# Attention features and an ELU block on one core: unread products at the start, one-bank tiles for h, and two token groups that take the weight pairs in turns

## The chip, the cores and the metric

The kernel runs on one core of one Trainium2 chip. The metric is the device time of one execution in microseconds (us). A core has five engines that run their own instruction streams: TensorE (PE in the rows; its weight loads are PEld), VectorE (DVE), ScalarE (ACT), GpSimd (POOL) and SyncE (SP, which here only issues transfers). Each works in the order in which its instructions stand, and waits on semaphores for the others.

## What is computed

The reference, cut to what matters (float64 weights `moe_w_in`, `moe_w_out`, `S1`, `S2`; q, k, v in float32):

```python
# batch, heads, seq, head_dim = 4, 4, 1088, 32;  r = 8;  d_model = 128, d_ff = 2048
def phi(x):
    a = einsum('rd,bhsd->bhsr', S1, x); b = einsum('rd,bhsd->bhsr', S2, x)
    return einsum('bhsi,bhsj->bhsij', a, b).reshape(..., r * r)
q_p, k_p = phi(q), phi(k)
kv  = einsum('bhsf,bhsd->bhfd', k_p, v);   z = sum(k_p, axis=s)
num = einsum('bhsf,bhfd->bhsd', q_p, kv);  den = einsum('bhsf,bhf->bhs', q_p, z) + 1e-06
x = (num / den) as (4352 tokens, 128)
h = x @ w_in
out = where(h > 0, h, exp(min(h, 0)) - 1) @ w_out
```

## The kernel before, in words

The 4352 tokens are 68 half tiles of 64; eight half tiles are a group of 512 tokens, so there are nine groups (0 to 8), the last with 256 tokens. Groups 0 and 1 belong to batch 0. `NP = 8` weight pairs (`cp`) hold 256 columns of `w_in` and the 256 rows of `w_out` that belong to them.

**The head** (code ahead of the list `steps`) loads k, q and v of batch 0, makes the features of k (`KF`, `KO`), sums k features times v into the PSUM tile `kv` (`KA`), makes the features of group 0 (`q1_first`, `q2_first`, `q4_first`) and the normalised x of group 0 (`q5_first`, tile `xg`). `q5_first` copies `kv` with its sum column into `kvz` (ScalarE), runs 16 products of 64 rows, one per head (`x0ps`), then DVE divides by the denominator (`dn`, `xn`), TensorE transposes (`x0tp`), and ScalarE and DVE copy one half of `xg` each. `keep_warm` issues a 128x128 product of the identity with itself into the tile `idle`, which nothing reads; six of them stand in `q5_first`.

**The weights** are float64 in DRAM. They land as pairs of 32-bit words in `raw` and are rounded to float32 by `round_a` (DVE), `round_b` (ScalarE) and `round_c` (four DVE instructions, or two DVE and two GpSimd with `pool=True`). `RA`, `RB`, `RC` do that for entry i of the list `order`: an entry is (pair, w_in?, w_out?). Before, the first four pairs are rounded in halves of 256 columns.

**The steps.** `seg` lists which group takes which pairs one after the other: before, group 0 takes pairs 0 to 3, group 1 pairs 0 to 3, group 0 pairs 4 to 7, group 1 pairs 4 to 7, and then each later group takes all eight. Step n is one (group, pair): `mm1` (two products of 512 tokens into the PSUM tile `h`, two banks, two buffers), `elu` (ScalarE: relu of -h, then exp, tile `e`; DVE: max(h, e - 1), tile `gg`), and two steps later `mm2` (two products accumulated in the PSUM tile `o`). When a stretch of pairs of a group ends, `fin1` copies `o` to `oT` or adds it there (DVE); after the last pair `fin2` transposes and stores. `at(n, ...)` puts other work after `mm1` of step n, `late(n, ...)` after `elu` of step n: rounding of the next weights, and for group g the steps `q1` (features and denominators, one PSUM tile), `q2` (DVE), `q4` (transposes, copied by ScalarE to `qpT`) and `q5` (products with `kvS`, copied to `xg`), and for each batch the k work. `KZ1` and `KZ2` fold a batch's sum of k features into the weights `SW` that `q1` of this batch needs; `KS` copies `kv` to `kvS`.

Each engine's program order is the order of this code. Transfers are issued by SP in the code's order, two of them and v of batch 0 by ScalarE.

Of the kernel before, what the change touches and what calls it, by code (L numbers as in the profile page):

```python
# [27 lines left out]
def kernel(  # L28
# [56 lines left out]

    ebias = const.tile([P, 1], F32, name="ebias")
# [18 lines left out]
    def round_c(raw, dst, pool=False):  # L105
        lo, hi = raw[:, :, 0], raw[:, :, 1]
# [3 lines left out]
        mant = lo.bitcast(F32)  # L110
        nc.vector.scalar_tensor_tensor(mant, lo, 2.0 ** -32, hi, op0=MUL, op1=ADD)  # L111
# [23 lines left out]
    load_v(nc.scalar, 0)  # L135
# [18 lines left out]
    order = [(0, 1, 0), (1, 1, 0), (2, 1, 0), (0, 0, 1), (3, 1, 0), (1, 0, 1), (2, 0, 1), (3, 0, 1)]  # L154
    order += [(cp, 1, 1) for cp in range(NP // 2, NP)]
# [25 lines left out]
    for b in range(1, B):  # L181
# [44 lines left out]
    kvz = const.tile([P, 2, D + 1], F32, name="kvz")  # L226
# [50 lines left out]
    def KZ1(b):  # L277
# [74 lines left out]

    WARM = 4, 2
    idle = psum.tile([P, 512], F32, name="idle", tag="o", bufs=1)

    def keep_warm():
        nc.tensor.matmul(idle[:, :P], ident[:], ident[:], skip_group_check=True)
# [28 lines left out]
    def q5_first():  # L386
        nc.scalar.copy(kvz[:], kv_ps[0][:, :, :D + 1])
# [8 lines left out]
        for i in range(WARM[0]):  # L396
            keep_warm()
# [17 lines left out]
        for i in range(WARM[1]):  # L415
            keep_warm()
# [231 lines left out]
```

## Time and profile before

| | |
|---|---|
| three runs | 320.78, 322.21, 322.82 us; median 322.21 |
| the profiled execution | 321.12 us, of which the profile's span is 318.6 us |
| TensorE busy | 296.2 us (93% of the span) |
| DVE, ScalarE, GpSimd busy | 160.4, 177.1, 22.5 us |
| mean granted TensorE clock | 0.989 of full speed |

Times in the rows are us from the span's start. A row of the timeline is: start, how long, engine, line, operation, out<-in tiles, shape, count of merged instructions, and in brackets how long the engine was idle before it and what released it. One float32 product is two TensorE rows, so "x4" of h or o is two products; a transpose is one row. The end of a TensorE row is modelled and lies beyond the start of the next one.

### The profile page before, as it was taken

How to read it: one execution, taken by the hardware profiler on the slowest of the kernel's cores; microseconds unless marked ns; L12 is line 12 of the kernel's file. 1: busy time of each engine (PE TensorE's matmuls, PEld its weight loads, DVE VectorE, ACT ScalarE, POOL GpSimd, SP SyncE). 2: the span in 40 equal slices, each digit the busy share in tenths (PEclk: the TensorE clock that was granted, in tenths of full speed). 3: DMA queues.
4: the chain of work that ended last, by engine and by line, in shares of the span. 5: the costliest groups of instructions: out<-in, count | busy, mean ns of one | idle time of the engine just before them, and what ended most of it. 6: DMA issues, size and time to landing. Idle time of an engine off the chain costs nothing. (4 is left out here: it accounts for less than half of the span.)

```text
span 318.6 us, 3773 instructions
## 1 busy us (share of the span) xinstructions
PE 296.2 (93%) x1498; PEld 151.3 (47%) x1498; DVE 160.4 (50%) x236; ACT 177.1 (56%) x237; POOL 22.5 (7%) x36
## 2 busy tenths in 40 slices
PE   2997769997999999999999999999999999999993
PEld 2863223543454444544554455444544444444682
DVE  5846865994533365446233645626333624443431
ACT  2326665554566565466655663566565565566561
POOL 2000014647000000000000000000000000000000
PEclk9997999997999999999999999999999999999999
DMA  6921189502001010000100010001000100010010
GB/s 187 337 83 30 39 228 255 146 0 70 0 2 33 0 33 2 0 2 0 34 2 0 0 33 2 0 2 34 0 2 0 33 0 0 2 33 0 0 35 16
DMA packets 9184, 13.34 MB, mean 42 GB/s; under 512 B 912, under 2 KB 6544, under 8 KB 9168
## 3 DMA queue, kind: packets, MB, share of 16 engines
q1 hardware_dynamic: 8336, 12.29, 14.0%
q10 hardware_dynamic: 832, 0.82, 0.9%
q8 instruction: 12, 0.20, 0.3%
q14 instruction: 4, 0.03, 0.0%
HBM read 10.88 MB, written 2.23 MB: 41 GB/s over the span
## 5 line engine op out<-in xcount | busy, mean ns | idle before, releaser
L473 DVE SCALAR_TENSOR_TENSOR gg<-e,h 128x1024 f32<-128x1024 f32 (+1 forms) x74 | 83.8, 1133 | 128.2 <-ACT e L472 123.6
L482 PE MATMUL o<-gg,W 128*128 128x512 f32 (+1 forms) x288 | 133.1, 585 | 4.0 <-POOL W L114 2.7
L460 PE MATMUL h<-xg,W 128*128 128x512 f32 (+1 forms) x288 | 130.4, 576 | 2.9 <-DVE gg L473 2.2
L471 ACT ACTIVATE e<-h 128x1024 f32<-128x1024 f32 (+1 forms) x74 | 70.9, 958 | 52.1 <-PE h L460 45.4
L460 PEld LDWEIGHTS h<-xg,W 128*128 128x128 f32 x288 | 54.3, 192 | 63.1 <-issue 61.7
L482 PEld LDWEIGHTS o<-gg,W 128*128 128x128 f32 x288 | 52.5, 192 | 57.5 <-issue 46.4
L472 ACT ACTIVATE e<-e 128x1024 f32<-128x1024 f32 (+1 forms) x74 | 73.1, 988 | 2.3
L240 ACT COPY ab<-abp 128x256 f32<-128x256 f32 (+1 forms) x12 | 3.7, 317 | 23.6 <-PE abp L236 23.6
L222 DVE TENSOR_TENSOR kp<-ab 128x1024 f32<-128x1024 f32 (+1 forms) x12 | 11.3, 953 | 7.8 <-ACT ab L240 7.8
L431 ACT COPY qpT<-qtp 128x512 f32<-128x512 f32 (+1 forms) x16 | 8.2, 562 | 12.1 <-PE qtp L430 12.1
L271 PEld LDWEIGHTS kv<-v,kp 128*64 128x64 f32 (+1 forms) x288 | 10.2, 147 | 7.7 <-issue 3.0
L271 PE MATMUL kv<-v,kp 128*64 128x33 f32 (+3 forms) x288 | 11.5, 235 | 0.3 <-DVE kp L222 0.3
L113 POOL TENSOR_TENSOR raw<-raw,tiny 128x512 f32<-128x512 f32 (+1 forms) x6 | 7.3, 1224 | 51.2 <-DVE raw L111 47.3
L333 ACT COPY abw<-abwp 128x384 f32<-128x384 f32 (+1 forms) x8 | 3.7, 457 | 12.8 <-PE abwp L328 12.8
L430 PEld LDWEIGHTS qtp<-ident,qp 128*128 128x128 f32 x60 | 7.0, 141 | 5.4 <-issue 3.7
L349 DVE TENSOR_TENSOR qp<-an,abw 128x1024 f32<-128x1024 f32 (+1 forms) x8 | 9.3, 1158 | 0.3
L450 ACT COPY xg<-xps 128x256 f32<-128x256 f32 (+1 forms) x8 | 2.9, 360 | 11.0 <-PE xps L445 11.0
L445 PE MATMUL xps<-qpT,kvS 64*32 64x128 f32 (+2 forms) x200 | 8.7, 298 | 0.2 <-ACT qpT L431 0.2
L236 PE MATMUL abp<-Sab,kT 128*64 128x64 f32 x136 | 7.8, 250 | 1.1 <-DVE kT L216 1.0
L430 PE MATMUL qtp<-ident,qp 128*128 128x128 f32 x60 | 7.9, 273 | 0.9 <-DVE qp L349 0.9
L236 PEld LDWEIGHTS abp<-Sab,kT 128*64 128x64 f32 x136 | 6.3, 159 | 3.7 <-DVE kT L216 2.2
L328 PEld LDWEIGHTS abwp<-SW,qT 128*64 128x64 f32 x120 | 5.4, 136 | 5.5 <-issue 5.3
(78 smaller groups left out, 136.2 us busy)
## 6 DMA issues: line engine op xcount, KB each, us to landing
raw<-in_moe_w_in_dram SPq DMA_DIRECT2D x8, 256.0 KB, 6.6
raw<-in_moe_w_out_dram SPq DMA_DIRECT2D x8, 256.0 KB, 5.3
out_dram<-osb SPq DMA_DIRECT2D x13, 128.0 KB, 2.3
hd_k<-in_k_dram SPq DMA_DIRECT2D x3, 544.0 KB, 10.9
hd_q<-in_q_dram SPq DMA_DIRECT2D x3, 544.0 KB, 9.4
v<-in_v_dram SPq DMA_DIRECT2D x3, 288.0 KB, 11.4
v<-in_v_dram SPq DMA_DIRECT2D x3, 256.0 KB, 8.3
hd_k<-in_k_dram SPq DMA_DIRECT2D x1, 288.0 KB, 3.3
```

The lines of the kernel that those rows point to most:

```text
L222: nc.vector.tensor_mul(dst, _ap(a_, list(a_.ap[1:]) + [[0, R]]), _ap(b_, [b_.ap[1], [0, R], b_.ap[2]]))
L236: nc.tensor.matmul(abp[64 * u:64 * u + 64, j * 64:j * 64 + 64], kT[b][:, u * KT + i, :], Sab[:].rearrange("p h y -> p (h y)"), skip_group_ ...
L271: nc.tensor.matmul(kv[64 * hp:64 * hp + 64, g2, :n], kp[:rows, j, h].rearrange("p i j -> p (i j)"), _ap(vt[b][:rows, off:off + D], [[VN - ...
L349: nc.vector.tensor_mul(qp[g][:, :m], _ap(a_, list(a_.ap[1:]) + [[0, R]]), _ap(b_, [b_.ap[1], [0, R], b_.ap[2]]))
L430: nc.tensor.transpose(p[:, o:o + P], qp[g][:, r:r + 2].rearrange("p t i j -> p (t i j)"), ident[:])
L431: nc.scalar.copy(qpT[g][:, 2 * hh:2 * hh + 2, :nh, :], p[:, :2 * nh * P].rearrange("p (h m s) -> p h m s", h=2, m=nh))
L445: nc.tensor.matmul(xp[w][D * h:D * h + D, :nh * P].rearrange("p (m s) -> p m s", s=P)[:, m0:m0 + m, s], kvS[64 * w:64 * w + 64, b, h, :], ...
L460: nc.tensor.matmul(h[:, c, :n], W[:, cp, c * P:c * P + P], xg[g][:, :n])
L471: nc.scalar.activation(e[:, c, :n], h[:, c, :n], RELU, scale=-1.0)
L472: nc.scalar.activation(e[:, c, :n], e[:, c, :n], EXP, scale=-1.0)
L473: nc.vector.scalar_tensor_tensor(gg[:, c, :n], e[:, c, :n], -1.0, h[:, c, :n], op0=ADD, op1=MAX)
L482: nc.tensor.matmul(ops[g][:, :n], W[:, cp, (2 + c) * P:(3 + c) * P], gg[:, c, :n], start=(first and c == 0), stop=(last and c == 1))
```

## The change

1. `keep_warm(n)` multiplies a tile of zeros (new, cleared by DVE first) instead of the identity. Ten such products stand ahead of the first real product, six ahead of the first k features; `q5_first` holds 2 and 2 where it held 4 and 2.
2. v of batch 0 is issued by SP, between q's first part and the weights; before, ScalarE issued it.
3. `order` rounds pair 0 in two halves and every other pair whole (512 columns). `round_c` is cut in three (`round_c`, `round_d`, `round_e`) with the same instructions.
4. `q5_first` multiplies `kv` by a mask into `kvz` with the two heads of a pair side by side and zeros in the other head's rows (one DVE instruction), and then needs 8 products of 128 rows and 66 columns. `KZ1`, `KZ2` and `q1(1)` move from the steps into it.
5. `h` is one bank per tile with four buffers (the same four banks), and `elu` always works in two halves.
6. Groups 0 and 1 take turns by 2, 2 and 4 pairs. `q2`, `q4`, `q5` of group 1 move to steps 0 and 1; the rounding of the later pairs is laid out anew; where the first stretch of a group ends ScalarE copies `o`.

```diff
+    zeros = const.tile([P, P], F32, name="zeros")
+    nc.vector.memset(zeros[:], 0.0)
...
-    def round_c(raw, dst, pool=False):
-        lo, hi = raw[:, :, 0], raw[:, :, 1]
+    def round_c(raw, dst):
+        hi = raw[:, :, 1]
         d = dst.bitcast(U32)
         nc.vector.scalar_tensor_tensor(d, hi, 0x80000000, d, op0=AND, op1=OR)
         nc.vector.tensor_scalar(hi, hi, 0x000FFFFF, 0x00100000, op0=AND, op1=OR)
...
+    def round_d(raw, dst):
+        lo = raw[:, :, 0]
+        nc.vector.scalar_tensor_tensor(lo.bitcast(F32), lo, 2.0 ** -32, raw[:, :, 1], op0=MUL, op1=ADD)
...
-    load_v(nc.scalar, 0)
+    load_v(nc.sync, 0)
...
-    order = [(0, 1, 0), (1, 1, 0), (2, 1, 0), (0, 0, 1), (3, 1, 0), (1, 0, 1), (2, 0, 1), (3, 0, 1)]
-    order += [(cp, 1, 1) for cp in range(NP // 2, NP)]
+    order = [(0, 1, 0), (1, 1, 1), (0, 0, 1)] + [(cp, 1, 1) for cp in range(2, NP)]
...
+    def keep_warm(n):
+        for i in range(n):
+            nc.tensor.matmul(idle[:, :P], zeros[:], zeros[:], skip_group_check=True)
...
     def q5_first():
-        nc.scalar.copy(kvz[:], kv_ps[0][:, :, :D + 1])
-        p = psum.tile([P, 2, 512], F32, name="x0ps", tag="h")
...
+        kv_ = kv_ps[0][:, :, :D + 1]
+        nc.vector.tensor_mul(kvz[:], _ap(kv_, [kv_.ap[1], [0, 2], kv_.ap[2]]), _ap(hmask[:], [[0, 2], [1, 2], [0, D + 1]]))
+        KZ1(0)
+        round_w(round_d, 0)
...
+            for m in range(4):
+                t, g2 = 2 * tt + m // 2, m % 2
+                nc.tensor.matmul(p[:, 2 * m * (D + 1):2 * (m + 1) * (D + 1)], qpT[0][:, t, g2, :],
+                                 kvz[:, g2].rearrange("p w d -> p (w d)"), skip_group_check=True)
+            if tt == 0:
+                KZ2(0)
+        round_w(round_e, 0)
+        q1(1)
+        keep_warm(WARM[0])
...
-        h = psum.tile([P, 2, 512], F32, name="h", tag="h")
+        hs[g, cp] = [psum.tile([P, 512], F32, name="h", tag="h", bufs=4) for c in range(2)]
...
-    seg = [(g, range(c, c + NP // 2)) for c in (0, NP // 2) for g in range(2)]
+    seg = [(g, r) for r in (range(0, 2), range(2, 4), range(4, NP)) for g in range(2)]
...
+    at(0, q2, 1)
+    at(0, RA, 2)
+    late(0, RB, 2)
+    late(0, KS, 0)
+    at(1, RC, 2)
+    at(1, q4, 1)
+    late(1, q5, 1)
+    for n, i in ((2, 3), (3, 4), (5, 5), (6, 6), (8, 7), (9, 8)):
+        at(n - 1, RA, i)
+        late(n - 1, RB, i)
+        at(n, RC, i, i > 4)
```

TensorE, from the products of group 0's x on, before. `x0ps` and `x0tp` belong to `q5_first`, `wps` to `KZ2`, `abwp` to `q1(1)`, `qtp` to `q4(1)`:

```order
L394 MATMUL x0ps<-kvz,qpT 128x33 x16
L357 MATMUL idle<-ident 128x128 x4
L413 MATMUL x0tp<-ident,xn 128x128 x4
L357 MATMUL idle<-ident 128x128 x2
L460 MATMUL h<-xg,W 128x512 x2
L288 MATMUL wps<-zm,SX 128x32
L460 MATMUL h<-xg,W 128x512 x2
L328 MATMUL abwp<-SW,qT_77 64x96 x8
L460 MATMUL h<-xg,W 128x512 x2
L482 MATMUL o<-gg,W 128x512 x2
L460 MATMUL h<-xg,W 128x512 x2
L430 MATMUL qtp<-ident,qp 128x128 x8
```

The same place of the changed program (`xps` is `q5(1)`):

```order
L424 MATMUL x0ps<-kvz,qpT 128x66 x4
L319 MATMUL wps<-zm,SX 128x32
L424 MATMUL x0ps<-kvz,qpT 128x66 x4
L359 MATMUL abwp<-SW,qT_77 64x96 x8
L212 MATMUL idle<-zeros 128x128 x2
L443 MATMUL x0tp<-ident,xn 128x128 x4
L212 MATMUL idle<-zeros 128x128 x2
L489 MATMUL h<-xg,W 128x512 x4
L459 MATMUL qtp<-ident,qp 128x128 x8
L474 MATMUL xps<-qpT,kvS 32x256 x8
L489 MATMUL h<-xg,W 128x512 x2
L509 MATMUL o<-gg,W 128x512 x2
```

`wps` and `abwp` moved ahead of the first h, `qtp` and `xps` moved from behind the fourth pair of h to behind the second.

DVE, from the copy of group 0's x on, before (L95, L108, L109, L111 and L116 are the rounding):

```order
L418 COPY xg<-x0tp 128x256
L282 TENSOR_TENSOR zm<-kv,zmask 128x32
L108 SCALAR_TENSOR_TENSOR W<-raw,W 128x256
L109 TENSOR_SCALAR raw<-raw 128x256
L111 SCALAR_TENSOR_TENSOR raw<-raw 128x256
L116 SCALAR_TENSOR_TENSOR W<-raw,W 128x256
L289 TENSOR_TENSOR SW<-wps,bmask 128x4x8
L95 TENSOR_SCALAR W<-raw 128x256
```

And in the changed program (the rounding is L97, L110, L111, L115 and L123 there; the rows from `pw` to `qp` are `q2(1)`):

```order
L447 COPY xg<-x0tp 128x256
L97 TENSOR_SCALAR W<-raw 128x512
L110 SCALAR_TENSOR_TENSOR W<-raw,W 128x512
L111 TENSOR_SCALAR raw<-raw 128x512
L115 SCALAR_TENSOR_TENSOR raw<-raw 128x512
L123 SCALAR_TENSOR_TENSOR W<-raw,W 128x512
L371 TENSOR_TENSOR pw_198<-abw 128x16x8
L373 TENSOR_REDUCE den<-pw_198 128x16
L374 RECIPROCAL den<-den 128x16
L376 TENSOR_TENSOR an<-abw,den 128x128
L380 TENSOR_TENSOR qp<-an,abw 128x1024
L97 TENSOR_SCALAR W<-raw 128x256
```

All of pair 1's rounding now stands between group 0's x and `q2(1)`, and `q2(1)` ahead of the first `gg`.

ScalarE, in the changed program, from the end of step 0's exp to group 1's x (L102 is `round_b`, L498 and L499 are relu and exp of step 1):

```order
L102 ACTIVATE W<-W,ebias 128x256
L328 COPY kvS<-kv 64x2x32 x4
L460 COPY qpT<-qtp 128x512 x2
L498 ACTIVATE e<-h 128x512
L499 ACTIVATE e<-e 128x512
L498 ACTIVATE e<-h 128x512
L499 ACTIVATE e<-e 128x512
L479 COPY xg<-xps 128x2x128
```

Before, `xg` of group 1 stood directly behind `qpT`, ahead of the relu of its step.

## Rows read from the trace of the kernel before

**Rows 1.** Windows, TensorE: stretch, its length, busy (rows), clock, DMA share, GB/s.
```profile
0.00:21.20 21.20, 14.40 (x183) 1.00 0.75 228
21.20:70.17 48.97, 41.52 (x212) 0.97 0.42 113
...
90.00:300.00 210.00, 208.90 (x979) 1.00 0.04 9
```

**Rows 2.** Waits of TensorE over the span: sum in us, times, longest.
```profile
PE o L482 <- POOL W L114: 2.7, 2, 2.5
PE h L460 <- DVE gg L473: 2.2, 1, 2.2
```

**Rows 3.** Windows, TensorE, around three of its waits (columns as in group 1).
```profile
28.20:31.70 3.50, 3.50 (x5) 0.51 0.21 55
...
43.50:46.00 2.50, 0.04 (x1) 1.00 0.90 240
46.00:72.40 26.40, 25.74 (x154) 1.00 0.53 138
...
76.00:79.40 3.40, 3.40 (x7) 0.50 0.00 0
```

**Rows 4.** Timeline, TensorE, head and first steps.
```profile
13.26 1.72 PE L383 MATMUL qtp<-ident,qp 128*128 128x128 f32 x8
...
16.76 1.98 PE L394 MATMUL x0ps<-kvz,qpT 64*128 64x33 f32 x32 [0.31 <-ACT kvz L387]
...
21.20 1.96 PE L460 MATMUL h<-xg,W 128*128 128x512 f32 x4 [0.16 <-DVE zm L282]
...
22.99 0.30 PE L288 MATMUL wps<-zm,SX 128*128 128x32 f32 x2
...
25.02 0.88 PE L328 MATMUL abwp<-SW,qT 128*64 128x96 f32 x16
...
36.87 1.09 PE L430 MATMUL qtp<-ident,qp 128*128 128x128 f32 x8 [0.86 <-DVE qp L349]
```

**Rows 5.** Timeline, SP's queue and DVE in the head.
```profile
5.63 1.20 SPq L76 DMA_DIRECT2D hd_q<-in_q_dram  x1
...
14.04 0.77 DVE L216 STREAM_TRANSPOSE qT<-hd_q 128x576 f32<-128x576 f32 x1
...
18.78 0.17 DVE L399 TENSOR_SCALAR dn<-x0ps 128x16 f32<-128x16 f32 x1 [3.79 <-PE x0ps L394]
```

**Rows 6.** DMA issues: tile, queue, count, KB, us from issue to landing.
```profile
hd_q<-in_q_dram SPq DMA_DIRECT2D x1, 288.0 KB, 7.5
```

**Rows 7.** Timeline, DVE and ScalarE: rounding of 512 columns.
```profile
53.58 0.42 DVE L95 TENSOR_SCALAR W<-raw 128x512 uint32<-128x512 uint32 x1
...
53.91 0.69 DVE L108 SCALAR_TENSOR_TENSOR W<-raw,W 128x512 uint32<-128x512 uint32 x1
...
54.63 0.43 DVE L109 TENSOR_SCALAR raw<-raw 128x512 uint32<-128x512 uint32 x1
...
55.68 0.71 ACT L100 ACTIVATE W<-W,ebias 128x512 uint32<-128x512 uint32 x1
```

**Rows 8.** Timeline, DVE and ScalarE: ELU halves and group 1's features.
```profile
28.50 0.63 ACT L472 ACTIVATE e<-e 128x512 f32<-128x512 f32 x1
...
29.63 0.68 DVE L473 SCALAR_TENSOR_TENSOR gg<-e,h 128x512 f32<-128x512 f32 x1
...
31.91 0.85 ACT L297 COPY kvS<-kv 64x64 f32<-64x64 f32 x4
...
37.56 1.07 ACT L431 COPY qpT<-qtp 128x512 f32<-128x512 f32 x2
...
79.86 0.28 DVE L340 TENSOR_TENSOR pw<-abw 128x128 f32<-128x128 f32 x1
...
81.13 1.22 DVE L349 TENSOR_TENSOR qp<-an,abw 128x1024 f32<-128x1024 f32 x1
```

**Rows 9.** Timeline, TensorE, the last products of the program.
```profile
312.63 1.13 PE L482 MATMUL o<-gg,W 128*128 128x256 f32 x4 [0.34 <-DVE gg L473]
```

More of the change, by code (lines that the diff above doesn't have):

```diff
@@ L161, in round_w, with RA, RB, RC @@
             f(raw_w[cp][:, c], W[:, cp, c], *a)
-    RA, RB, RC = ((lambda i, *a, f=f: round_w(f, i, *a)) for f in (round_a, round_b, round_c))
+    def RA(i):
+        round_w(round_a, i)
+    def RB(i):
+        round_w(round_b, i)
+    def RC(i, pool=False):
+        round_w(round_c, i)
+        round_w(round_d, i)
+        round_w(round_e, i, pool)
     load_w(0, 0)
     load_w(1, 0)
+    load_w(1, 1)
     load_w(0, 1)
-    load_w(1, 1)
     load_hd(nc.sync, "q", q, 0, 8, NT)
@@ L225 @@
     kvS = const.tile([P, B, H, D], F32, name="kvS")
-    kvz = const.tile([P, 2, D + 1], F32, name="kvz")
+    kvz = const.tile([P, 2, 2, D + 1], F32, name="kvz")
     kv_ps, feats, zms = {}, {}, {}
@@ L350, in q2 @@
                              _ap(b_, [b_.ap[1], [0, R], b_.ap[2]]))
[L353 to L357, printed above, removed]
+    WARM = 2, 2
     def q1_first():
@@ L411, in q5_first @@
             for t in range(2):
-                r = 4 * tt + 2 * t
-                nc.tensor.transpose(q[:, t * P:t * P + P], xn[:, r:r + 2].rearrange("p m w d -> p (m w d)"), ident[:])
+                nc.tensor.transpose(q[:, t * P:t * P + P], xn[:, tt, 4 * t:4 * t + 4].rearrange("p m d -> p (m d)"), ident[:])
             xt.append(q)
-        for i in range(WARM[1]):
-            keep_warm()
+        keep_warm(WARM[1])
         nc.scalar.copy(xg[0][:, :256], xt[0][:, :256])
@@ L485, with fin1 @@
     oT = {}
-    def fin1(g):
+    def fin1(g, last):
         n = qn[g] * P
@@ L493, in fin1 @@
             oT[g] = work.tile([P, 512], F32, name="oT", tag="oT")
-            nc.vector.tensor_copy(oT[g][:, :n], o)
+            (nc.vector.tensor_copy if last else nc.scalar.copy)(oT[g][:, :n], o)
     def fin2(g):
@@ L550, in late @@
         extra.setdefault((n, 1), []).append((f, *a))
-    at(0, KZ2, 0)
-    at(0, RA, 3)
-    at(0, RC, 2)
-    late(0, RB, 3)
-    at(1, q1, 1)
-    at(1, RA, 4)
-    at(1, RC, 3)
-    late(1, RB, 4)
-    late(1, KS, 0)
-    at(2, RC, 4)
-    at(2, q2, 1)
-    at(2, RA, 5)
-    late(2, RB, 5)
-    at(3, RC, 5)
-    at(3, RA, 6)
-    at(3, q4, 1)
-    at(3, q5, 1)
-    late(3, RB, 6)
-    for n in range(4, 10):
-        i = n + 2
-        if i + 1 < len(order):
-            at(n, RA, i + 1)
-            late(n, RB, i + 1)
-        at(n, RC, i, True)
+    at(0, q2, 1)
[9 more added lines that the diff above has]
+        at(n, RC, i, i > 4)
     for b in range(1, B):
```

78 lines of the change are left out of this document (38 added, 40 removed).

## The prediction, made before the changed kernel ran

> **What bounds the kernel now.** I read the table of windows first. From 90 to 300 us TensorE is busy 208.90 of 210.00 us at full clock [rows 1]: there the kernel is as fast as its products, and no other engine's work counts as long as it stays hidden. What can be won lies ahead of that. Up to the first product of h at 21.20 [rows 4] the head makes group 0's x. From 21.20 to 70.17, ten steps long, TensorE is busy 41.52 of 48.97 us [rows 1], so it idles 7.45 us. The table of waits names the largest: 2.7 us for a rounded weight (GpSimd finishing W), 2.2 us for an h buffer that `gg` had not freed [rows 2]; the timeline has some ten waits there in all. The clock rows add a second cost: after the wait of 2.2 us TensorE was granted half speed from about 28.2 to 31.7, in which its rows do half the work, 1.7 us lost; after a wait of like length ahead of batch 1's `wps` the same from 76.0 to 79.4; after the 2.5 us of idle time up to 46.0 the clock stayed full [rows 3]. So two of three such waits drew a half-speed stretch of some 3.4 us. The clock column reads 1.00 for the whole head, but eight transposes took 1.72 us at 13.26 and 1.09 us at 36.87 [rows 4]: the head's first rows ran at 1.2 GHz too, 0.215 us each.
>
> **The head.** The ten unread products are 20 rows, at 0.215 us [rows 4] 4.3 us from about 1.0 to 5.3 if they run at 1.2 GHz throughout; the six more are 2.6 us, or half of that once the clock is up. That holds the first k features back by 1 to 3 us. I cost this at nothing, because of what covers it: DVE must transpose the second part of q before `kvz` in its order, and that part lands at 13.1 (issued 5.63 [rows 5], 7.5 us to landing [rows 6]). v's move to SP's queue leaves the bytes ahead of it the same. If the k chain ended later than DVE gets to `kvz`, the cover would be gone and the difference would come on top: up to 1 us, in the range.
>
> From 13.1: transposes 0.77 [rows 5] to 13.9; two rounding steps of 256 columns, about 0.35 each by rather more than half of the 512-column rows [rows 7], to 14.6; `kvz` is not in the trace, the nearest row is the 128x128 product at 0.28 [rows 8], below it nothing, so 14.9. The 8 products of paired heads have 16 rows of full height where before 32 rows of half height ran two by two in 1.98 us [rows 4]: as a load of 128 columns goes with each of the 16 as with each of the 16 pairs, I take the same 1.8 to 2.0, and the `wps` rows between them 0.2: end at 17.0. `q1(1)`, 0.88 [rows 4], and two unread products fit while DVE divides. From `dn` to the first h it took 21.20 - 18.78 = 2.4 [rows 4, 5], with one more small DVE row 2.6. First h at 19.6: **-1.6 us**. Bounds: 19.0 if q's second part comes earlier, now that no second queue mixes v into it, and 21.2 if it comes later or the k chain is late.
>
> The Trainium skill ("TensorE: Matmul & The Clock Gate", Part 1) says that half rate is the default, that activity lifts it, and that the point where it changes is not tied to the kernel's start, so that a count of slow products from one run should not be fitted to another. By that rule the clock may come up anywhere from soon after the unread products to the k features, and first h would lie anywhere from 19.5 to 21.2 rather than at one value; the trace, one execution, cannot show the spread.
>
> `wps` and `q1(1)` stood behind the first h and now stand ahead of it: TensorE has 0.2 and 0.9 us less to do afterwards [rows 4]: **-1.1 us**.
>
> **The first ten steps.** Before, group 0 went through four pairs in its first four steps. A pair costs DVE about 2.9 us of rounding (0.42 + 0.69 + 0.43 + 0.69 + 0.69 [rows 7]) and 1.4 us of `gg` (two halves of 0.68 [rows 8]), 4.3 us against 3.4 us of TensorE (four products, two of them in 1.7 from 21.20 on [rows 4]): DVE was late, and TensorE waited for W. With two pairs for two groups a pair is needed only every second step, 2.9 + 2.8 us of DVE against 6.9 us. I expect the waits for W and for h buffers to be gone from the third step on.
>
> In their place group 1's x is needed after two steps, and its whole chain is open. Counted from the first h (t = 0), when DVE has copied `xg`:
> - the second pair's h waits for pair 1's rounding: 0.42 + 0.71 + 0.69 + 0.43 + 0.69 + 0.69 [rows 7] and hand-overs, 3.8. The last of these is not in the trace at 512 columns; its kind is 0.69. The first pair ends at 1.7: idle 2.1.
> - `q2(1)` follows on DVE, 79.86 to 82.35 before, 2.5 [rows 8]: `qp` at 6.3, the second pair's h ends at 5.5: idle 0.8.
> - transposes to 7.2. ScalarE has ahead of `qpT`: rounding of 256 columns, about 0.5 where 512 take 0.71 [rows 7] (after DVE's 0.3 behind `qp`), `kvS` 0.85, then 1.07 for both halves of `qpT` [rows 8]: 7.1, 7.9, 9.0. Idle about 1.3 and 0.3, products of x to 9.5.
> - group 1's `xg` stands on ScalarE behind four halves of relu and exp of 0.63 [rows 8], to 11.6; DVE's half of it behind the last `gg` half 0.68, and about 0.4 itself: 12.7. Idle 3.1.
>
> Together 7.6 us from start to start. A row's modelled end lies 0.17 beyond the next row's start (21.20 + 1.96 against 22.99 [rows 4]), so this is 6.8 us idle, with 0.3 for the short wait on batch 1's features that stays 7.1, against 7.45. Five or six waits instead of ten also save that edge of nearly 0.2 each time, about 0.8. Half speed: before one stretch, 1.7; after, the wait of 3.1 with the 1.6 ahead of it should draw one, the 2.1 may draw another; I take 1.7, and 1.7 more in the range. Sum **-1.2 us**.
>
> **The rest.** ELU in halves costs ScalarE at most 4 x 0.63 and DVE 2 x 0.68 us a step [rows 8]; both lie under 3.4 us of TensorE. Two more additions of `o` are hidden likewise, and the wait ahead of batch 1's `wps` stays with its half-speed stretch [rows 3]: the same DVE queue stands ahead of it. **0**, and 1.7 either way for the clock. At the end, the last two products waited 0.34 for a whole `gg` [rows 9]; in halves the first of them no longer waits and runs beside the second half's exp: half of the 0.86 between the two products' start and end, and most of the 0.34: **-0.7 us**.
>
> Sum -1.6 - 1.1 - 1.2 - 0.7 = -4.6 against the profiled execution's 321.12, so 316.5; the three runs stand around it (median 322.21). Single edits in the unknown direction (small waits that the one-bank tiles end early) lean to the fast side; I say **316.0**.
>
> **Rivals.**
> - *Both new waits are shorter and the one ahead of batch 1's `wps` draws no half speed*: DVE's rounding of pair 1 overlaps more, the clock holds: another 3 to 5 us less, 311 to 313. For it: the clock held after one wait of 2.5 [rows 3].
> - *The head gains nothing*: q's second part lands 1.5 us later since SP now issues v ahead of the weights, first h at 21.1, and each of the two new waits draws half speed: 316.0 + 1.5 + 1.7 = 319.2, to 320.5 with a third. Against it: the same bytes lie ahead of q's second part either way. The Trainium skill ("DMA: Bandwidth & Descriptors", "Issuing engines are not separate DMA queues") says that both issuers run on the same 16 DMA engines; by that rule v's move changes no landing time in the sum. No row shows v issued on SP in the head.
> - *Slower: products of zeros do not lift the clock.* The place is the head. Then 32 unread rows cost 6.9 us at 0.215 without giving anything, the k features start at 8.7 and run at half speed up to x: products of paired heads 3.6 instead of 1.8, `q1(1)` and transposes double, first h near 24.6 and its first steps at half speed: +3.4 + 1.7 against before, less 1.1 and 0.7, with two half-speed stretches more 1.7 to 3.4: 325 to 327. It decides if the clock has not risen by the products of x. Against it: in the trace the unread products of the identity ran at full speed where they were; no row shows zeros.
> - *It does not do what it says*: x's products at 66 columns and full height cost as much as before, which the sum holds already.
>
> **Chances.** Forecast (313 to 319) 0.62, the faster case 0.18, the head gains nothing 0.15, slower 0.05. About 1% (3.2 us) is what a measurement of this kernel can tell from no change: below 319.0 faster, above 325.4 slower. Forecast and the faster case lie below 319.0: faster 0.80; the third, and a part of the last, within: 0.16; slower 0.04. Range 310.5 to 320.5: it leaves out the slower case and what lies past the ends of the others; the forecast's own is 313 to 319.
>
> **What would show it.** Right: first h between 19 and 21 with `kvz` right behind the q transposes and two rounding rows; TensorE waiting about 2 us for DVE's last rounding row before the second pair, about 3 us for `xg` before group 1's first h, and hardly for W after that; the last o products without a wait. Wrong: abp rows (k features) that end after 10 us and a late `kv`; clock rows at 0.5 in three or more stretches; ScalarE's copy of `o` or the split `gg` ending TensorE's waits between 90 and 300.

## The result, and the profile after

The changed kernel takes 313.01 us (median of four executions, 312.70 to 314.22) against 322.51 for the kernel before beside it. The ratio is 0.9708, with a 95% interval of 0.9642 to 0.9775: faster by nearly 3%. It lies in the predicted range, 3 us below the predicted 316.0. The profiled execution took 314.22 us, with a span of 312.4. A ratio leaves out executions that are over 1.5% longer than the fastest of their kernel, so it need not be the quotient of the medians beside it (run 6 below).

TensorE in the windows of the changed kernel that answer to [rows 1] and to the stretch around batch 1's `wps` (columns as there; stretch, length, busy, clock, DMA share, GB/s):

```profile
0.00:21.66 21.66, 19.26 (x212) 1.00 0.71 223
21.66:68.18 46.52, 39.41 (x194) 0.96 0.48 119
68.18:74.43 6.25, 5.52 (x35) 1.00 0.28 89
90.00:300.00 210.00, 209.23 (x966) 1.00 0.04 9
```

The second window runs from the first h to the h of step 10, as the second of [rows 1] does. In the first, the clock column reads 1.00, as it did before, although the length of rows shows half speed there (2.93 us in the first row below, 1.60 in run 1). TensorE's timeline in the same execution, the rows that answer to [rows 3] and [rows 4] (start, how long, engine, line, operation, tiles, idle time ahead and its releaser):

```profile
6.76 2.93 PE L212 MATMUL idle<-zeros 128*128 128x128 f32 x12
...
16.97 1.08 PE L424 MATMUL x0ps<-kvz,qpT 128*128 128x66 f32 x8 [0.49 <-DVE kvz L415]
...
21.66 1.96 PE L489 MATMUL h<-xg,W 128*128 128x512 f32 x4 [0.16 <-DVE xg L447]
25.30 1.98 PE L489 MATMUL h<-xg,W 128*128 128x512 f32 x4 [1.68 <-DVE W L123]
27.86 1.07 PE L459 MATMUL qtp<-ident,qp 128*128 128x128 f32 x8 [0.58 <-DVE qp L380]
29.87 1.15 PE L474 MATMUL xps<-qpT,kvS 64*32 64x256 f32 x16 [0.94 <-ACT qpT L460]
33.82 3.03 PE L489 MATMUL h<-xg,W 128*128 128x512 f32 x4 [2.79 <-DVE xg L480]
36.64 2.54 PE L509 MATMUL o<-gg,W 128*128 128x512 f32 x4
...
71.14 0.38 PE L319 MATMUL wps<-zm,SX 128*128 128x32 f32 x2 [0.73 <-DVE zm L313]
...
72.61 1.98 PE L509 MATMUL o<-gg,W 128*128 128x512 f32 x4
...
304.49 2.75 PE L509 MATMUL o<-gg,W 128*128 128x256 f32 x12
307.76 0.44 PE L527 MATMUL otp<-ident,oT 128*128 128x128 f32 x2 [0.52 <-DVE oT L521]
```

The reader is to see four waits behind the first h (1.68, 0.58, 0.94 and 2.79 us), one half-speed stretch behind the last of them (3.03 and 2.54 us for rows that take 1.9), a wait of only 0.73 ahead of batch 1's `wps` with rows at full speed behind it, and last o products that wait for nothing.

The kernel before, at batch 1's `wps`, on TensorE:

```profile
74.62 0.38 PE L288 MATMUL wps<-zm,SX 128*128 128x32 f32 x2 [2.21 <-DVE zm L282]
...
76.09 3.63 PE L482 MATMUL o<-gg,W 128*128 128x512 f32 x4
79.56 1.88 PE L460 MATMUL h<-xg,W 128*128 128x512 f32 x4
```

From such rows the profiled executions divide as follows. The last column is the same changed kernel run once more (first experiment).

| stretch of TensorE's work | before | predicted | after | again |
|---|---|---|---|---|
| start to the first h | 21.20 | -1.6 | 21.66 (+0.46) | 19.57 (-1.63) |
| first h to the h of step 10 | 48.97 | -2.3 | 46.52 (-2.45) | 47.30 (-1.67) |
| step 10 to the first h behind batch 1's wps | 9.39 | 0 | 6.25 (-3.14) | 6.27 (-3.12) |
| from there to the last two products of h | 229.98 | 0 | 229.19 (-0.79) | 229.19 (-0.79) |
| from there to the last transposes | 4.74 | -0.7 | 4.14 (-0.60) | 4.13 (-0.61) |
| to the end of the span | 4.32 | 0 | 4.64 (+0.32) | 4.64 (+0.32) |

The figures of the columns "after" and "again" are times, with the difference from before in brackets. The differences sum to -6.2 and -7.5 us of span. Two of the lines (first h to step 10, and the tail) came within 0.6 us of their forecast. One was predicted as zero and is the largest. The first has two values for one program.

### The profile page after: what moved, and what is told of

Read it like the earlier page. It is cut to its first block, busy times and chain, and to the rows that moved or that the text cites. A ratio compares the mean times of both kernels' runs of the same rounds, so it can differ in the third digit from the quotient of the medians.

```text
span 312.4 us, 3991 instructions
## 1 busy us (share of the span) xinstructions
PE 296.7 (95%) x1510; PEld 155.0 (50%) x1510; DVE 170.2 (54%) x297; ACT 195.4 (63%) x375; POOL 19.6 (6%) x32
## 4 chain that ended last, share of the span: by engine, by line
PE 83%; DVE 10%; ACT 4%; issue 2%; DVEq 0%
PE o L509 36%; PE h L489 33%; PE idle L212 3%; PE xps L474 2%; PE abwp L359 2%; DVE gg L500 2%; PE qtp L459 2%; DVE kp L248 2%; PE kv L297 2%; DVE W L110 1%; PE abp L262 1%; PE otp L527 1%; ACT e L499 1%; DVE raw L111 1%; ACT e L498 1%
## 5 line engine op out<-in xcount | busy, mean ns | idle before, releaser
L500 DVE SCALAR_TENSOR_TENSOR gg<-e,h 128x512 f32<-128x512 f32 (+1 forms) x144 | 93.4, 655 | 109.0 <-ACT e L499 108.9
L509 PE MATMUL o<-gg,W 128*128 128x512 f32 (+1 forms) x288 | 131.3, 580 | 0.0
L498 ACT ACTIVATE e<-h 128x512 f32<-128x512 f32 (+1 forms) x144 | 81.5, 566 | 18.9 <-PE h L489 18.5
L499 ACT ACTIVATE e<-e 128x512 f32<-128x512 f32 (+1 forms) x144 | 87.3, 606 | 4.6
L248 DVE TENSOR_TENSOR kp<-ab 128x1024 f32<-128x1024 f32 (+1 forms) x12 | 12.2, 1025 | 12.1 <-ACT ab L266 12.1
L297 PE MATMUL kv<-v,kp 128*64 128x33 f32 (+3 forms) x288 | 10.7, 225 | 0.6 <-DVE kp L248 0.6
L212 PE MATMUL idle<-zeros 128*128 128x128 f32 x40 | 8.9, 402 | 1.1 <-DVE warm L139 1.1
L529 ACT COPY osb<-otp 128x512 f32<-128x512 f32 (+1 forms) x9 | 5.1, 563 | 6.8 <-PE otp L527 6.8
L102 ACT ACTIVATE W<-W,ebias 128x512 uint32<-128x512 uint32 (+1 forms) x9 | 6.0, 666 | 4.8 <-DVE W L97 4.8
L212 PEld LDWEIGHTS idle<-zeros 128*128 128x128 f32 x40 | 8.0, 302 | 1.4 <-DVE warm L139 1.1
```

The source lines that it names most:

```text
L212: nc.tensor.matmul(idle[:, :P], zeros[:], zeros[:], skip_group_check=True)
L248: nc.vector.tensor_mul(dst, _ap(a_, list(a_.ap[1:]) + [[0, R]]), _ap(b_, [b_.ap[1], [0, R], b_.ap[2]]))
L297: nc.tensor.matmul(kv[64 * hp:64 * hp + 64, g2, :n], kp[:rows, j, h].rearrange("p i j -> p (i j)"), _ap(vt[b][:rows, off:off + D], [[VN - ...
L498: nc.scalar.activation(e[:, c, :n], h[c][:, :n], RELU, scale=-1.0)
L499: nc.scalar.activation(e[:, c, :n], e[:, c, :n], EXP, scale=-1.0)
L500: nc.vector.scalar_tensor_tensor(gg[:, c, :n], e[:, c, :n], -1.0, h[c][:, :n], op0=ADD, op1=MAX)
```

## The experiments

All ratios are to the kernel before on the same chip; four to ten executions each. "Theory" and "rival" are those of the expectation that stands with the run.

**1. The changed kernel again.** No edit.

> The changed kernel itself, unchanged, beside the three others of this set. Its profiled execution had its first h at 21.66 us with a span of 312.4; three other executions had spans of 310.9 to 311.4. If the head varies from run to run (where in it the clock rises), the first h should come at another time here, between 20 and 22, and the rest from the first h to the end stay at 290.7 within 0.7. If the head is the same each time, first h is at 21.6 again and the spread lies behind it. Ratio to the kernel before about 0.971 either way.

Measured: 312.68 us, ratio 0.9708 (0.9660 to 0.9755). TensorE in the head:

```profile
6.43 1.60 PE L212 MATMUL idle<-zeros 128*128 128x128 f32 x12
...
14.88 1.08 PE L424 MATMUL x0ps<-kvz,qpT 128*128 128x66 f32 x8 [0.49 <-DVE kvz L415]
...
19.57 1.96 PE L489 MATMUL h<-xg,W 128*128 128x512 f32 x4 [0.16 <-DVE xg L447]
```

The six unread products ahead of the k features took 1.60 us here and 2.93 in the other execution: here they ran at full speed, in the other execution at half. All that follows moves with it, and the first h comes 2.1 us sooner, earlier than the 20 to 22 expected. So the head has no single time. Behind the first h the two executions agree but for 0.8 us, which lies in where the half-speed stretch falls.

**2. No unread products at the start.**

```diff
-    keep_warm(10)
...
-    keep_warm(6)
```

> The changed kernel without the ten unread products ahead of the first real one and without the six ahead of the first k features (the 2 and 2 beside the products of x stay). Theory A: the sixteen products pay for themselves and no more: the first k features came at 9.62 us with them against 5.69 before, but the clock was up some 4 us sooner, so eight transposes took 1.06 us instead of 1.72 and the first k-times-v block 1.15 instead of 1.98; without them the k features start near 6 and run at half speed, and the first h stays within 0.7 us of 21.6: ratio about 0.971 as with them. Rival B: the delay is pure loss, since the last k-times-v block waits for the k features and the unread products push those back by 2 us: first h at 19.7, ratio 0.965. Rival C: without them the clock rises only in the first steps: first h at 23 or later and half-speed rows behind it: ratio 0.978 or more.

Measured: 311.85 us, ratio 0.969 (0.9653 to 0.9728). TensorE and DVE in the head:

```profile
5.86 1.62 PE L261 MATMUL abp<-Sab,kT 128*64 128x64 f32 x16 [0.48 <-DVE kT L241]
...
19.40 1.95 PE L488 MATMUL h<-xg,W 128*128 128x512 f32 x4 [0.16 <-DVE xg L446]
```

```profile
12.95 0.78 DVE L241 STREAM_TRANSPOSE qT<-hd_q 128x576 f32<-128x576 f32 x1 [0.75 <-DMA hd_q<-in_q_dram]
```

The ratio is theory A's (0.965, rival B's, lies just outside the interval), and so are the k features: they start at 5.86 and run at half speed (1.62 us for rows that take 0.69 elsewhere). The first h at 19.40 is not where A had it (20.9 to 22.3) but near B's 19.7. It does not decide, since run 1 had it at 19.57 with the products. DVE waits here for the landing of q's second part, as the prediction had it. The sixteen products gave nothing that the time shows.

**3. Two-bank tiles, elu whole.**

```diff
-        hs[g, cp] = [psum.tile([P, 512], F32, name="h", tag="h", bufs=4) for c in range(2)]
+        hs[g, cp] = psum.tile([P, 2, 512], F32, name="h", tag="h")
...
-        for c in range(2):
+        parts = 2 if (g, cp) in ((0, 0), (0, 1)) else 1
+        for c in range(parts):
```

> The changed kernel with h back in tiles of two banks, two of them, and elu in one piece from the third step on (the first two steps in halves, as before the change); x of group 0 takes one such tile. Theory A: the halves are what freed DVE and TensorE around batch 1's wps: the wait ahead of it (0.73 us after, 2.21 before) and the half-speed stretch behind it (1.7) come back, +3.1, the four waits of some 0.15 to 0.2 for a whole gg behind q1 come back, +0.7, and the last two products, +0.6: 4.4 us more than with the change, ratio 0.984. Rival B: the wait shrank because GpSimd's rounding held fewer DVE rows up (one 1.5 and one 1.8 us row before, against 0.4 and 0.7 elsewhere); then only +1.3 comes back: ratio 0.975.

Measured: 318.43 us, ratio 0.9943 (0.9902 to 0.9984): 5.7 us slower than the changed kernel on the same chip, more than either theory gave, and for another reason. The wait ahead of batch 1's `wps` did not come back: it is 0.39. What came is in the first steps. ScalarE (L501 is the relu), then TensorE:

```profile
28.29 0.60 ACT L501 ACTIVATE e<-h 128x512 f32<-128x512 f32 x1 [3.65 <-DVE gg L503]
```

```profile
31.36 1.59 PE L475 MATMUL xps<-qpT,kvS 64*32 64x256 f32 x16 [2.69 <-ACT qpT L461]
36.17 3.75 PE L490 MATMUL h<-xg,W 128*128 128x512 f32 x4 [3.22 <-DVE xg L481]
```

The relu of step 0's second half stood idle for 3.65 us until DVE's `gg` of the first half was done, and that stood behind pair 1's rounding and `q2(1)`. The two halves lie in different banks, but in one tile, and the program makes the second reader of the tile wait. With one-bank tiles ScalarE goes on, although `e` is one tile for both halves there too: so it is h's tile that holds the relu up. Behind it `qpT` and group 1's x are late (waits of 2.69 and 3.22 instead of 0.94 and 2.79); batch 1's k transposes are late too (1.84 instead of 1.1, by the table of waits). The Trainium skill ("PSUM — Partial Sum Buffer", "PSUM bank collisions raise a hardware error") says that two engines that touch one bank and the same partitions have to be kept apart, reads against reads too. By that rule two different banks need no such wait: the tile, not the bank, is what the program guarded here.

**4. Turns of 4 and 4 pairs.**

```diff
-    seg = [(g, r) for r in (range(0, 2), range(2, 4), range(4, NP)) for g in range(2)]
+    seg = [(g, r) for r in (range(0, NP // 2), range(NP // 2, NP)) for g in range(2)]
...
-    for n, i in ((2, 3), (3, 4), (5, 5), (6, 6), (8, 7), (9, 8)):
+    for n, i in ((1, 3), (2, 4), (4, 5), (5, 6), (7, 7), (8, 8)):
```

> The changed kernel with groups 0 and 1 in turns of 4 and 4 pairs again, q2, q4 and q5 of group 1 back at steps 2 and 3, and the rounding laid out for that (pair 1 and pair 0's second half by step 1, then pairs 2 and 3 whole by steps 1 and 2, the later ones from step 4 on); head, h tiles and elu as changed. Theory A (the prediction's): DVE needs 4.3 us a pair where TensorE needs 3.4, so TensorE waits for W of pairs 2 and 3 again, 2 to 3 us, and what 2-2-4 costs (waits of 1.68, 0.58, 0.94 and 2.79 us and a half-speed stretch of 1.7 in the profiled execution) is saved in part only: 0 to 2 us slower than the changed kernel, ratio 0.971 to 0.977. Rival B: the four waits of 2-2-4 cost more than the waits for W that they replace, now that the head and the halves of elu leave DVE more room: 1 to 3 us faster than the changed kernel, ratio 0.962 to 0.968.

Measured: 313.27 us, ratio 0.9735 (0.9686 to 0.9785). TensorE's waits for W are there as theory A said:

```profile
23.20 1.98 PE L489 MATMUL h<-xg,W 128*128 128x512 f32 x4 [1.69 <-DVE W L123]
29.05 2.97 PE L489 MATMUL h<-xg,W 128*128 128x512 f32 x4 [3.86 <-DVE W L123]
...
35.58 1.98 PE L489 MATMUL h<-xg,W 128*128 128x512 f32 x4 [1.14 <-DVE W L123]
```

They sum to 6.69 us with one half-speed stretch; the four waits of 2, 2 and 4 sum to 5.99 with one such stretch. So the turns, each with the rounding laid out for them, exchange one set of waits for another of the same size. From the first h to step 10 this kernel takes 46.98 us, the changed one 46.52 and 47.30. Any gain of the turns is within what this can resolve.

**5. Both undone: the head and the whole-pair rounding are left.** The edits of 3 and 4 together.

> The changed kernel with two of its parts undone together: turns of 4 and 4 pairs, and h in two two-bank tiles with elu whole from the third step on. What is left of the change is the head (unread products of zeros, v on SP, x from 8 products, KZ and q1(1) ahead of the first h) and the rounding in whole pairs. Theory A, from the two runs that undid one part each: the turns gave nothing (0.9735 with 4 and 4 against 0.9708 with 2, 2, 4, the intervals overlap), the tiles and halves gave nearly 6 us (0.9943 without them); so this is about 3 us faster than the kernel before, head 1.6 and moved work 1.1: ratio 0.990, and batch 1's wps waits some 2 us again with half-speed rows behind it. Rival B: the two-bank tiles were dear only under 2-2-4, where the relu of one half waited 3.65 us for DVE's gg of the other behind the rounding; with 4 and 4 they cost only the stretch at batch 1's wps and the tail, 2 to 4 us on 313.3: ratio 0.978 to 0.984.

Measured: 317.19 us, ratio 0.9876 (0.9824 to 0.9929): between the theories, nearer to A. The waits for W are larger than in 4 (8.3 us in sum, the longest 5.4). But the wait ahead of batch 1's `wps` is 0.39 and no half speed follows, against A's expectation:

```profile
72.44 0.38 PE L319 MATMUL wps<-zm,SX 128*128 128x32 f32 x2 [0.39 <-DVE zm L313]
```

**6. One-bank tiles and halves alone, in the kernel before.**

```diff
-        h = psum.tile([P, 2, 512], F32, name="h", tag="h")
+        h = [psum.tile([P, 512], F32, name="h", tag="h", bufs=4) for c in range(2)]
...
-            elu(g, cp, 2 if n < 2 else 1)
+            elu(g, cp)
```

> The kernel before with one part of the change alone: h in four one-bank tiles and elu in halves in every step. x of group 0 then takes two one-bank tiles, so its denominators are two DVE rows and its division goes by head pair, up to 0.4 us more in the head. Theory A: the tiles and halves carry more than half of the gain by themselves: the wait of 2.2 us for an h buffer that gg had not freed, and its half-speed stretch of 1.7, go; 1 to 2 us of the wait ahead of batch 1's wps and the 1.7 behind it; 0.7 in the four waits behind q1 and 0.6 at the end: 5 to 7 us, ratio 0.979 to 0.985. Rival B: alone they save only the tail and the four waits, since DVE's rounding in four steps is what TensorE waits for in the kernel before: 1 to 1.5 us, ratio 0.995 to 0.997.

Measured: 315.84 us (311.75 to 317.23), ratio 0.9759 (0.9636 to 0.9882): theory A rather than B, and more than A's 0.979 to 0.985. The interval is wide, since the ratio rests on two executions, 311.75 and 315.00 us; it holds the changed kernel's 0.9708 too. The profiled execution is the longest of the four. Its first h is at 23.13, with half-speed rows late in its head, so it is read from there on:

```profile
23.13 1.96 PE L458 MATMUL h<-xg,W 128*128 128x512 f32 x4
...
27.89 1.98 PE L458 MATMUL h<-xg,W 128*128 128x512 f32 x4
...
67.94 1.88 PE L458 MATMUL h<-xg,W 128*128 128x512 f32 x4
...
72.45 0.38 PE L288 MATMUL wps<-zm,SX 128*128 128x32 f32 x2 [2.28 <-DVE zm L282]
...
73.91 3.52 PE L479 MATMUL o<-gg,W 128*128 128x512 f32 x4
```

The wait of 2.2 us for an h buffer [rows 2] and the half-speed stretch behind it [rows 3] are gone: the h of step 2 starts at once. From the first h to step 10 it takes 67.94 - 23.13 = 44.81 us instead of 48.97. That is less than the changed kernel's 46.52, although `wps` and `q1(1)` still stand in this stretch here: no half-speed rows fell in it, and TensorE idled 5.26 us instead of 7.11. The wait ahead of batch 1's `wps` and its half-speed stretch are still there, which theory A had expected to shrink. So the tiles are not what removed those.

**7. Halves on shared tiles.** As 3, with `parts = 2` everywhere.

> The changed kernel with h back in two two-bank tiles, but elu in halves in every step. Theory A: a half on a shared tile is no half: in the run with two-bank tiles the relu of the second half stood idle until DVE's gg of the first half was done (3.65 and 0.75 us in the first two steps). So relu 0.60, exp 0.63 and gg 0.69 of both halves follow one another, with hand-overs some 4.0 us a step against TensorE's 3.43; with two buffers TensorE then waits in every step: some 0.5 us in 64 steps and less in the last 8, 25 to 40 us more, ratio 1.06 to 1.10. Rival B: that wait is an effect of DVE's queue in the first steps alone; later ScalarE and DVE stay hidden and the halves give what they give with one-bank tiles (the four waits behind q1 and the tail): ratio 0.975 to 0.992.

Measured: 335.32 us, ratio 1.0457 (1.0387 to 1.0527): theory A's mechanism at a lower price, 22 us more than the changed kernel where 25 to 40 were expected. ScalarE's waits by releaser (sum, times, longest), and below it the relu of the first step's second half in the kernel before, which halves two steps:

```profile
ACT e L501 <- DVE gg L503: 71.7, 72, 4.0
```

```profile
25.95 0.60 ACT L471 ACTIVATE e<-h 128x512 f32<-128x512 f32 x1 [1.50 <-DVE gg L473]
```

There is one such wait for each of the 72 steps. Halving the elu gains only because the halves are tiles of their own.

**8. Group 1's x ahead of the elu, no unread products at the start.**

```diff
-    late(1, q5, 1)
+    at(1, q5, 1)
```

> The changed kernel without the sixteen unread products at the start, and with q5 of group 1 (the products of x and their copies) ahead of the elu of step 1 on ScalarE and DVE instead of behind it. Theory A: group 1's first h waits for its copied x, which stands behind four halves of relu and exp (2.5 us on ScalarE) and two of gg; ahead of them it is ready some 2.3 us sooner, the wait of 2.8 falls to about 0.5, and the half-speed stretch behind it (1.7) may go with it: 2.3 to 4 us less than without the unread products alone (0.969), ratio 0.956 to 0.962. Rival B: what is behind it comes late instead, since gg of step 1 frees the h tiles and feeds the o products two steps on: TensorE waits there for as long, ratio 0.967 to 0.971.

Measured: 309.73 us (309.14 to 310.42), ratio 0.9639 (0.9572 to 0.9707): between the theories, nearer to A. All its executions are below all eight of the changed kernel (311.77 to 314.22) and all four of run 2 (311.37 to 312.22), but on another chip, and the intervals of the ratios overlap. TensorE:

```profile
30.68 1.95 PE L488 MATMUL h<-xg,W 128*128 128x512 f32 x4 [0.69 <-DVE xg L479]
```

The wait of 2.79 is 0.69 (A had about 0.5), and here no half-speed rows follow. The first h was at 20.61 in this execution, so the gain was not in the head. This is the lowest time of the study.

**9. The later pairs' rounding without a gap.**

```diff
-    for n, i in ((2, 3), (3, 4), (5, 5), (6, 6), (8, 7), (9, 8)):
+    for n, i in ((2, 3), (3, 4), (6, 5), (7, 6), (8, 7), (9, 8)):
```

> The changed kernel with pairs 4 to 7 finished at steps 6, 7, 8 and 9 instead of 5, 6, 8 and 9, which fills the one step (7) in which DVE has no rounding; nothing else is moved. Theory A: what shrank the wait ahead of batch 1's wps (2.21 us before, 0.73 after) is the layout of the rounding: before, DVE rounded in each of steps 4 to 9 and had no gap from 61.5 us to that wps; in the two runs with turns of 4 and 4, which finish the pairs a step earlier still, the wait was 0.39, with whole and with halved elu. With the later layout it grows to 1.5 to 2.5 us, and if the clock falls behind it 1.7 more are lost: 0.8 to 3.5 us slower than the changed kernel, ratio 0.973 to 0.982. Rival B: the halves and one-bank tiles did it and DVE takes the fuller step without delay: 0.971.

Measured: 314.36 us, ratio 0.9732 (0.9682 to 0.9782). The intervals overlap; the trace decides:

```profile
69.89 0.38 PE L319 MATMUL wps<-zm,SX 128*128 128x32 f32 x2 [1.26 <-DVE zm L313]
...
71.84 3.14 PE L509 MATMUL o<-gg,W 128*128 128x512 f32 x4
```

The wait is 1.26 instead of 0.74, a little under what A said, and the half-speed stretch is back: from `wps` to the next h 4.93 us instead of 3.29. The wait of 1.1 for the k transposes, ahead of which the changed kernel rounds a pair, is gone in return.

**10. No rounding on GpSimd.** `at(n, RC, i, i > 4)` becomes `at(n, RC, i)`.

> The changed kernel with the last rounding row of pairs 4 to 7 on DVE (one row of 0.69 us a pair) instead of two GpSimd rows. Theory A: DVE has 0.69 us more in each of four steps and nothing back: the wait ahead of batch 1's wps grows from 0.73 to 1.5 to 2.2 us, with or without a half-speed stretch of 1.7: ratio 0.973 to 0.981. Rival B: DVE gets more back than it gives, since its rows are slow where GpSimd's run beside them (1.64, 1.25 and 1.40 us from 48.7 to 53.0 in the first repeated run, against 0.69, 0.43 and 0.70 for the same rows elsewhere): the waits for the k transposes (1.1) and ahead of wps (0.73) shrink: ratio 0.966 to 0.970. If the slow rows stay slow, GpSimd's copy of v, which is left where it is, holds them up, and not its rounding.

Measured: 315.38 us, ratio 0.9773 (0.9721 to 0.9824): theory A. The wait ahead of `wps` is 1.99 and the o products behind it take 3.50:

```profile
73.35 0.38 PE L319 MATMUL wps<-zm,SX 128*128 128x32 f32 x2 [1.99 <-DVE zm L313]
...
74.82 3.50 PE L509 MATMUL o<-gg,W 128*128 128x512 f32 x4
```

**11. Version 8 with pairs 6 and 7 a step earlier.** `(8, 7), (9, 8)` becomes `(7, 7), (8, 8)`.

> The version that was fastest so far (no unread products at the start, q5 of group 1 ahead of the elu of step 1) with pairs 6 and 7 finished at steps 7 and 8 instead of 8 and 9. Theory A: DVE comes sooner to batch 1's sum of k features, the wait of 0.72 us ahead of wps falls to 0.4 or less as in the runs with 4 and 4: 0.3 to 0.7 us less, ratio 0.961 to 0.963. Rival B: step 7 fills with rounding beside k features and GpSimd's copy of v, so k features of batch 1 come later and the gain goes into waits for kp: ratio 0.964 to 0.966.

Measured: 312.07 us, ratio 0.967 (0.9631 to 0.9708): rival B or worse. The wait ahead of `wps` is 0.87, and TensorE now waits 0.96 for `kp`, batch 1's k features. Its profiled execution also drew half speed behind the same 0.69 us wait as version 8:

```profile
30.82 3.63 PE L488 MATMUL h<-xg,W 128*128 128x512 f32 x4 [0.69 <-DVE xg L479]
```

The two traces divide the loss. Of the 2.5 us between their spans (308.6 and 311.1), 1.68 lie between the start of this half-speed row and the next h. Another 0.64 lie between that h and the first h behind `wps`, where the wait for `kp` is, and 0.15 in the head. So the layout loses some 0.6 us, as B said, and the clock the rest.

**12. v of batch 0 on ScalarE's queue.** `load_v(nc.sync, 0)` becomes `load_v(nc.scalar, 0)`.

> The changed kernel with v of batch 0 issued by ScalarE again. Theory A: v issued by ScalarE runs beside q's first part and behind the first weights: q's first part landed 5.3 us after its issue before and 4.5 after, v 7.1 us after its issue before and 5.3 after. With v on ScalarE DVE waits for q's first part again (1.0 us in the kernel before, nothing after), and the k features behind it on DVE and TensorE come up to 1 us later; the first h comes 0.8 to 1.6 us later than in the runs whose clock rises alike (19.57): 20.4 to 21.2, ratio 0.973 to 0.976. Rival B, the prediction's: the same bytes stand ahead of q's second part either way and the sixteen unread products hold the k features back longer than the transfers do: first h within 0.4 us, ratio 0.971.

Measured: 312.87 us, ratio 0.9709 (0.9662 to 0.9757): rival B. q's two parts land 5.6 and 7.2 us after their issue (4.5 and 6.5 in run 1), and the first h is at 19.80 instead of 19.57. So v's queue does move q's landings, by 1.1 and 0.7 us, where the prediction had no change; next to none of it reaches the first h.

## Why the prediction was right, and where it was not

**The head, -1.6.** Its steps hold where the clock rises early: `x0ps` was to start at 14.9 and did at 14.88, the first h was to come at 19.6 and came at 19.57. That is partly luck. The cover that the step named was q's second part, which DVE would wait for. In run 1 that part landed at about 12.55 (6.05 + 6.5), and DVE transposed it at 13.06, behind its rows for the k features, with no idle time from 9.11 on. Only without the unread products did DVE wait for it (run 2), and `kvz` came at 14.28 instead of 14.44. In the other profiled execution of the changed kernel `x0ps` started at 16.97: the six unread products ran at half speed to their end, the k features came 2.1 us later on TensorE and on DVE, and nothing covered them. The prediction allowed 1 us for that, with 21.2 as its bound for the first h; it cost 2.1. Costing the unread products at nothing was right in the time (run 2), and costing v's move at nothing was right within 0.3 us (run 12). What then made the head shorter than before was not tested. One candidate that the prediction and the list of the change pass over is the product for `SXps`, which the change moved too: in the kernel before it stands right ahead of the first k-times-v block, and now at the start, where TensorE waits for k anyway. Its row on TensorE before:

```profile
10.61 0.76 PE L211 MATMUL SXps<-Sx,idr 8*128 8x128 f32 x2 [0.38 <-ACT ab L240]
```

That is up to 1.1 us, an estimate from this row and its wait; it is argued, not shown.

**First h to step 10, -2.3.** The chain of new waits was read rightly: 2.1, 0.8, 1.3 and 3.1 were expected, 1.68, 0.58, 0.94 and 2.79 came, with one half-speed stretch as taken. The sum was off by 0.2 to 0.6. Idle time was forecast at 7.1 us in sum and is 46.52 - 39.41 = 7.11, by luck: the four waits came 0.8 shorter than forecast, and the wait for batch 1's k transposes, put at 0.3, was 1.11. The reason behind the gain was wrong. The prediction credited the end of the waits for W and h buffers to the turns; run 4 shows that the turns are worth nothing that can be measured, and runs 3 and 6 that the one-bank tiles with the halves are worth some 6 us. In this stretch alone run 3 takes 52.34 us instead of 46.52, and run 6 takes 44.81 instead of 48.97 with the old turns. The sum came out since the step let ScalarE run relu and exp of one half behind the other, which only these tiles allow.

**Batch 1's wps, 0.** This is the step that failed: "the same DVE queue stands ahead of it". It is not the same queue. Before, DVE rounded in every step from 4 to 9; after, step 7 has only a pair's first row (0.51 us) and pairs 2 and 3 are done by step 3. DVE and GpSimd in the kernel before and, below it, in the changed kernel:

```profile
68.09 1.29 POOL L114 TENSOR_TENSOR W<-raw,W 128x512 f32<-128x512 f32 x1
68.15 1.78 DVE L108 SCALAR_TENSOR_TENSOR W<-raw,W 128x512 uint32<-128x512 uint32 x1
...
74.31 0.17 DVE L282 TENSOR_TENSOR zm<-kv,zmask 128x32 f32<-128x32 f32 x1
```

```profile
63.57 2.16 POOL L121 TENSOR_TENSOR W<-raw,W 128x512 f32<-128x512 f32 x1
...
65.69 0.68 DVE L110 SCALAR_TENSOR_TENSOR W<-raw,W 128x512 uint32<-128x512 uint32 x1
...
70.83 0.17 DVE L313 TENSOR_TENSOR zm<-kv,zmask 128x32 f32<-128x32 f32 x1
```

Counted from the h of step 10 (70.17 and 68.18), `zm` came after 4.14 us before and 2.65 after: 1.5 us less wait, and 1.65 us less behind it because the clock stayed up. Filling step 7 (run 9), or giving DVE 0.69 us more a pair (run 10), brings a longer wait and the half speed back; the tiles alone (run 6) leave both; whole-pair rounding with two-bank tiles (runs 3 and 5) has neither. So it is the layout of the rounding, and the traces divide the 1.5 us. DVE began its last rows ahead of `zm`, from the `gg` of step 8 on, 0.53 us sooner; run 9 gives just that back (3.18 instead of 2.65). The same rows then took 0.96 us less, since the row above took 0.68 where it took 1.78: before, GpSimd worked on its own rounding product beside it, and after, that product had ended. Run 6, which keeps the old layout, has that row at 1.71. No run moves this meeting alone, so its part rests on the rows. The prediction had the new order in front of it and did not count DVE's rows between steps 7 and 10 as it did between 0 and 3.

The clock behind this wait: in nine profiled executions it was 0.39 to 0.87 us and full speed followed, in five (before, runs 6, 7, 9, 10) 1.26 to 4.10 and half speed followed. At group 1's first h a wait of 0.69 drew half speed once (run 11), so a short wait is no assurance. Nor need a long one draw half speed each time: the fastest execution of run 6, which was not traced, has a mean granted clock of 1.000.

**The steady part, 0; measured -0.79.** It goes with the tiles and halves: without them (run 3) that stretch takes 229.97 us, 0.8 longer again. The prediction left it out, though it named "small waits that the one-bank tiles end early" as the direction.

**The tail, -0.7; measured -0.60.** Right: the last o products no longer wait [rows 9], and with whole elu (run 3) the wait of 0.34 is back.

**The rivals.** The faster case, 311 to 313, named this wait and the clock behind it, and took part of the result: its second half came true, its first hardly (1.68 and 2.79 where 2.1 and 3.1 were expected). "The head gains nothing" came true in one profiled execution, for another reason than the one given. The slower case did not occur: the clock had risen by the products of x in both profiled executions of the changed kernel.

## What to carry to other kernels

Count the rows of the engine that ends a wait ahead of every wait, not only ahead of the first ones, and look at what GpSimd does beside them: where the rounding stood in steps 4 to 9 was worth 3.1 us here with the clock behind it, more than the 1.7 to 2.5 us of the first ten steps, which the change was read for. Two engines that read halves of one PSUM tile may be chained by the program although the halves lie in different banks; look for a reader that waits for another reader, which the kernel before showed already in its first two steps. Where a wait drew half-speed rows, about 1.7 us came on top of it, and one program had its first h at 19.57 and at 21.66: compare traces from the first h on.

## What the runs showed of the hardware that was not expected

**DVE beside GpSimd.** Rows that take 0.69 and 0.43 us alone (runs 1 and 10, the same rounding rows of one pair) take twice as long and more while GpSimd finishes a rounding product (48.48 to 49.78) and then copies v. Run 1, DVE and GpSimd, then run 10, where GpSimd is idle at that point:

```profile
48.71 1.64 DVE L110 SCALAR_TENSOR_TENSOR W<-raw,W 128x512 uint32<-128x512 uint32 x1
50.38 1.25 DVE L111 TENSOR_SCALAR raw<-raw 128x512 uint32<-128x512 uint32 x1
```

```profile
49.73 2.80 POOL L282 COPY v<-v 64x1152 f32<-64x1152 f32 x2
```

```profile
51.82 0.69 DVE L110 SCALAR_TENSOR_TENSOR W<-raw,W 128x512 uint32<-128x512 uint32 x1
52.54 0.43 DVE L111 TENSOR_SCALAR raw<-raw 128x512 uint32<-128x512 uint32 x1
```

In run 10 the copy of v falls later, from 61.25 to 64.05, and there two such rows on DVE take 1.52 and 1.43: so the copy alone is enough. The 1.78 us row of the kernel before, above, stood beside GpSimd's rounding. The Trainium skill ("SBUF — State Buffer", "Who interferes with whom") says that a DVE instruction with two SBUF inputs contends with a GpSimd instruction that reads SBUF, and that the port pair they share is an exclusive lock. The rows agree, and the row with one input (1.25) was slow too. Taking the rounding off GpSimd still lost (run 10): DVE had an extra row a pair, and the copy of v slowed other rows.

**The clock in the head.** In the nine profiled executions with the sixteen unread products (result, runs 1, 3, 4, 5, 7, 9, 10, 12) the first h came at 19.5 to 19.8 us six times and at 21.4 to 21.7 three times; in the three without them (runs 2, 8, 11) at 19.40, 20.61 and 20.76. The two means are alike, 20.3. The range that the prediction gave for it, 19.5 to 21.2, holds eight of the twelve. In run 8 rows ahead of the first h ran at half speed:

```profile
16.57 1.55 PE L358 MATMUL abwp<-SW,qT 128*64 128x96 f32 x16
```

The same row takes 0.88 in [rows 4]. So the first h is not where these products were to be judged by one trace. And one wait, two outcomes: behind 0.69 us ahead of group 1's first h, version 8 ran on at full speed (1.95 us) and version 11 at half (3.63).
